# Starting one batch's attention steps earlier and sending another batch's output through the DMA crossbar, in a fused attention and SwiGLU kernel

## The chip, the cores and the metric

The kernel runs on one core of one Trainium2 chip. The core has a matrix engine (PE, with its weight loads shown apart as PEld), a vector engine (DVE), a scalar engine (ACT), a general engine (POOL, GpSimd) and a queue engine (SP, SyncE) that here only issues DMAs. Each engine runs its own instructions in program order and waits for others by semaphores. Matmul results go to PSUM, eight banks per partition; DVE and ACT read them from there. The metric is device microseconds of one launch. The kernel before takes 372.36 us, the median of nine runs that lie between 371.16 and 373.12 us.

## What is computed

Eight batches of eight heads, sequence 576, head width 64: attention with a mask (a band of 32 positions to each side, and eight global positions that see and are seen by all), then a SwiGLU feed-forward block over all 4608 tokens:

```python
scores = scale * np.matmul(q, k.transpose(0, 1, 3, 2))
mask = (np.abs(pos[:, None] - pos[None, :]) <= 32) | is_global[:, None] | is_global[None, :]
attn = softmax(np.where(mask, scores, -1e9))
x = np.matmul(attn, v).transpose(0, 2, 1, 3).reshape(B * S, H * D)   # 4608 x 512
g = x @ w_gate                                                        # 512 -> 1536
out = (g * sigmoid(g) * (x @ w_val)) @ w_out                          # 1536 -> 512
```

Inputs and output are float32; the matmuls work on bf16.

## The kernel before, in words

**The feed-forward block sets the beat.** The 4608 tokens are cut into nine chunks of 512. A chunk is 16 units: twelve `gate` units (each four matmuls into `pg` and four into `pv`, line 704, then a tanh on ACT, line 735, and two DVE operations, `gv` and `h`, lines 737 and 741) and four `outp` units (twelve matmuls into `po`, line 748, a scaling copy on ACT, line 753, a DMA to the output, line 755). The last loop of the kernel runs these 144 units in order, and after unit n it runs the list `gaps[n]`. All attention work of batches 1 to 7, the loads of later batches and three pieces left over from batch 0 stand in these gaps. The program order so written is the order on every engine; nothing is reordered by a scheduler.

**One batch of attention** is a list of steps: `step_T(hp)` transposes k and q of a head pair on PE (batches 1 and 2 only; later batches are cast to bf16 in DRAM by `cast_qk` and transposed by a DMA, `transpose_qk`); `step_GT`, `step_SG`, `step_S2`, `step_P2T` and `step_AV2` handle the global positions; `step_S(u)` makes the scores of the band in five tiles (matmuls, line 492; exp on ACT, line 500; times the band on DVE, line 506, giving `pt`); `step_AV(tp)` multiplies by v in four tiles of 128 rows (lines 540 and 549) and then normalises on DVE (lines 521, 526, 527), giving `xa`; `step_AV8` does the last 64 rows; `step_X(tp)` and `step_X8` transpose `xa` into `xT`, the input of the feed-forward block. For batches below `XB` the transposes of `step_X` are PE matmuls (line 598, 617) and an ACT copy (604, 623); from `XB` on they are DMA transposes issued by SP (lines 587, 610). `xa` has three buffers.

**Where the steps stand.** Before the loop the whole of batch 0 runs, except `step_S(4)`, `step_AV8` and `step_X8`, which stand in gaps 0, 2 and 3. The first two gates of chunk 0 are computed in parts between batch 0's last steps. Batch 1 has its `step_T` in gaps 4, 5 and 6 (two in 6), its scores to `step_AV(0)` in gaps 7 to 11, `step_X(3)` in gap 15 with chunk 1 starting right behind it, `step_AV8` and `step_X8` in gaps 16 and 17. Batch 2 starts in gap 16 and ends in gap 30. Chunk 1 needs batch 1's tokens, chunk 2 needs the first three tiles of batch 2.

**PSUM.** Three pools share the eight banks: `pf` has four single banks (tag `f`: gates, outputs, and batch 0's small tiles), `psc` (tag `sc`) and `pm` (tag `m`) have one pair of two banks each. A step that takes a pair waits until the readers of the pair's last tile have finished. `step_S` uses `sc` except tile 2 of batch 0; `step_T` uses `sc` except `hp` 3; `mtile`, which serves `step_GT`, `step_P2T`, `step_AV2`, `step_X` and `step_X8`, is `m` for every batch but 0.

**Queues.** POOL issues all loads that cast (`load_qk_part`, `load_v`, `cast_qk`, the weights), the gathers of the global rows, and computes their masks (`gather_mask`). SP issues, in this order, batch 2's shifted copy of v (`load_vb`), batch 3's DMA transposes of k and q, and then chunk 1's four output DMAs.

## Time and profile before

| | us |
|---|---|
| median of nine runs | 372.36 |
| lowest, highest | 371.16, 373.12 |
| the profiled execution's own time | 370.23 |
| its span from the first to the last instruction | 368.5 |
| PE busy in the span | 351.0 |
| PE idle in the first 20 us, and from 20 to 40 us | 8.23, 2.77 |
| PE idle from 40 to 300 us, as the windows give it | 2.4 |
| last matmul's end to the end of the span | 4.0 |

The busy time of PE is an upper bound for its work, since matmuls overlap and their ends are modelled; starts are exact. In a timeline row the first number is the start, the second the length, then engine, line, operation, `output<-inputs`, shape, count; a bracket tells how long the engine was idle before the row and what ended it. "Gap n" below is the list after unit n; in this execution gap 2 lies at 32.7 us, gap 11 at 55.3, gap 15 at 69.4, gap 24 at 92.5, gap 30 at 111.3.

### The profile page before, as it was taken

To read this page: it belongs to the slowest core of one execution; us is meant where nothing else is said; L and a number is where in the kernel's file an instruction comes from. 1 tells how busy PE (TensorE), PEld (TensorE's weight loads), DVE (VectorE), ACT (ScalarE), POOL (GpSimd) and SP (SyncE) were. 2 spreads that over 40 slices of the span, in tenths; PEclk is the share of its full clock that TensorE was granted. 3 is DMA by queue.
4 is the path that set the end of the run, shared out by engine and by line. 5 is a ranking of instruction groups with operands and counts; after the bars stand their busy time and mean duration, and the time that the engine had idled before them with its cause. 6 is when DMAs were issued, how large, how long until landed. Compare 5 with 4: busy or idle time off the path is not lost.

```text
span 368.5 us, 7982 instructions
## 1 busy us (share of the span) xinstructions
PE 351.0 (95%) x3294; PEld 175.0 (47%) x3294; DVE 239.0 (65%) x473; ACT 152.7 (41%) x237; POOL 97.5 (26%) x114
## 2 busy tenths in 40 slices
PE   3788999999999999999999999999999999999995
PEld 2565545554454444444444454444544454444442
DVE  6676885288833885488548854886488637815840
ACT  5644573357423552255225532552254233323321
POOL 7947547570227002450246013200000000000000
PEclk9999999999999999999999999999999999999999
DMA  7999999999959996999999998932330131011002
GB/s 103 147 212 203 186 222 169 181 180 150 118 84 121 173 102 110 116 154 143 147 148 144 153 138 136 170 72 60 112 87 2 44 114 24 0 59 58 0 30 85
DMA packets 138996, 42.92 MB, mean 116 GB/s; under 512 B 123856, under 2 KB 133072, under 8 KB 138960
## 3 DMA queue, kind: packets, MB, share of 16 engines
q0 software_dynamic: 93824, 19.40, 64.0%
q1 hardware_dynamic: 45136, 23.01, 30.7%
q8 instruction: 26, 0.43, 0.5%
q14 instruction: 10, 0.08, 0.1%
HBM read 38.28 MB, written 15.34 MB: 145 GB/s over the span
## 4 chain that ended last, share of the span: by engine, by line
PE 84%; DVE 7%; ACT 3%; DMA 3%; issue 1%; POOL 0%; SPq 0%; DVEq 0%; POOLq 0%
PE po L748 26%; PE pg L704 23%; PE pv L704 22%; PE ps_av L540 3%; PE ps_s L492 2%; PE ps_av L549 2%; ACT pe L500 2%; DVE pt L506 2%; DMA vb<-va 2%; PE ps_t L374 1%; DMA k_bf<-in_k_dram 1%; DVE h L741 1%; DVE gvt L468 1%; DVE gv L737 1%; PE ps_x L598 1%
## 5 line engine op out<-in xcount | busy, mean ns | idle before, releaser
L704 PE MATMUL pg<-xT,wg_sb 128*128 128x512 bf16 x424 | 109.3, 380 | 1.2 <-ACT xT L604 0.7
L704 PE MATMUL pv<-xT,wv_sb 128*128 128x512 bf16 x424 | 108.8, 379 | 0.0
L735 ACT ACTIVATE th<-pg 128x512 bf16<-128x512 f32 x108 | 64.4, 597 | 81.6 <-PE pg L704 78.7
L748 PE MATMUL po<-wo_sb,h 128*128 128x512 bf16 x432 | 97.4, 380 | 0.0
L737 DVE SCALAR_TENSOR_TENSOR gv<-th,pg 128x512 bf16<-128x512 bf16 x108 | 74.0, 685 | 34.5 <-ACT th L735 33.9
L741 DVE TENSOR_TENSOR h<-gv,pv 128x512 bf16<-128x512 bf16 x108 | 74.3, 688 | 12.0 <-PE pg L704 0.5
L704 PEld LDWEIGHTS <-wv_sb 128*128 128x128 bf16 x424 | 41.5, 98 | 50.0
L102 POOL DMA_DIRECT2D va<-in_v_dram x40 | 35.1, 962 | 109.0 <-PE ps_av L549 80.4
L748 PEld LDWEIGHTS <-h 128*128 128x128 bf16 x432 | 40.8, 98 | 47.5
L704 PEld LDWEIGHTS <-wg_sb 128*128 128x128 bf16 x424 | 37.2, 98 | 42.0 <-issue 2.9
L753 ACT ACTIVATE osb<-po 128x512 f32<-128x512 f32 x36 | 21.5, 597 | 85.8 <-PE po L748 80.9
L500 ACT ACTIVATE pe<-ps_s 128x1024 bf16<-128x1024 f32 (+1 forms) x40 | 37.4, 939 | 17.2 <-PE ps_s L492 16.6
L506 DVE TENSOR_TENSOR pt<-pe,band 128x1024 bf16<-128x1024 bf16 (+1 forms) x40 | 25.5, 637 | 23.0 <-ACT pe L500 22.9
L521 DVE TENSOR_REDUCE den<-ps_av 128x8 f32<-128x16 f32 (+1 forms) x40 | 6.7, 169 | 36.7 <-PE ps_av L549 35.3
L527 DVE TENSOR_TENSOR xa<-ps_av,den 128x512 bf16<-128x512 f32 (+1 forms) x40 | 25.5, 638 | 1.4
L540 PE MATMUL ps_av<-gvt,pg 128*64 128x264 bf16 x128 | 18.1, 296 | 1.0 <-DVE gvt L476 1.0
L549 PE MATMUL ps_av<-vb,pt 128*64 128x66 bf16 x256 | 17.7, 198 | 1.2 <-DMA vb<-va 1.2
L549 PEld LDWEIGHTS <-pt 128*64 128x64 bf16 x512 | 17.6, 114 | 1.6 <-DMA vb<-va 1.4
L492 PEld LDWEIGHTS <-kT 64*128 64x128 bf16 x576 | 11.3, 98 | 14.4 <-issue 13.6
L549 PE MATMUL ps_av<-va,pt 128*64 128x66 bf16 x256 | 17.8, 198 | 0.0
L492 PE MATMUL ps_s<-qT,kT 64*128 64x64 bf16 x576 | 16.0, 197 | 0.0
L109 POOL DMA_DIRECT2D qf<-in_q_dram x5 | 14.1, 2826 | 0.0
(113 smaller groups left out, 219.8 us busy)
## 6 DMA issues: line engine op xcount, KB each, us to landing
out_dram<-osb SPq DMA_DIRECT2D x36, 256.0 KB, 2.0
vb<-va SPq DMA_DIRECT2D x14, 264.0 KB, 4.5
va<-in_v_dram POOLq DMA_DIRECT2D x24, 128.0 KB, 5.2
kf<-in_k_dram POOLq DMA_DIRECT2D x5, 576.0 KB, 13.1
qf<-in_q_dram POOLq DMA_DIRECT2D x5, 576.0 KB, 20.8
k_bf<-in_k_dram POOLq DMA_DIRECT2D x6, 288.0 KB, 11.9
q_bf<-in_q_dram POOLq DMA_DIRECT2D x6, 288.0 KB, 12.6
va<-in_v_dram POOLq DMA_DIRECT2D x16, 96.0 KB, 5.9
```

Of the source, the lines that this page charges most:

```text
L102: nc.gpsimd.dma_start(out=va[lo:hi, u, :, 0:D], in_=vs[t0 + lo : t0 + hi])
L492: nc.tensor.matmul(out=ps[:, par, 64 * slot : 64 * slot + 64], lhsT=kT[r : r + 64, hp, 64 * t : 64 * t + P], rhs=qTs[b][r : r + 64, hp, 64 ...
L500: nc.scalar.activation(out=pe, in_=ps[:, :, 0 : 64 * ns].rearrange("p r (s c) -> p r s c", c=64), func=AF.Exp, scale=SCALE,)
L506: mult = lambda: nc.vector.tensor_tensor(out=pt.rearrange("p r s c -> p (r s) c"), in0=pe.rearrange("p r s c -> p (r s) c"), in1=bc(band, ...
L527: nc.vector.tensor_tensor(out=xa.rearrange("p (g h) d -> p g h d", g=g), in0=bc(ps, pst + [[1, D]]), in1=bc(den, [[4, g], [1, 4], [0, D]]) ...
L540: nc.tensor.matmul(out=ps[64 * e : 64 * e + 64, hg], lhsT=st["pg"][:, P * tp + 64 * e : P * tp + 64 * e + 64], rhs=st["gv"].rearrange("p h ...
L549: nc.tensor.matmul(out=ps[64 * e : 64 * e + 64, hg, hl, :], lhsT=pt[:, hl % 2, 4 * (hl // 2) + 2 * (tp % 2) + e, :], rhs=(va if e == 0 els ...
L704: nc.tensor.matmul(out=ps[:, 0:n], lhsT=w[:, cc, P * fc : P * (fc + 1)], rhs=xT[:, cc, t0 : t0 + n], start=(cc == 0), stop=(cc == NCC - 1),)
L735: nc.scalar.activation(out=th[:, 0:n], in_=pg[:, 0:n], func=AF.Tanh, scale=0.5)
L737: nc.vector.scalar_tensor_tensor(out=gv[:, 0:n], in0=th[:, 0:n], scalar=1.0, in1=pg[:, 0:n], op0=ALU.add, op1=ALU.mult,)
L741: nc.vector.tensor_tensor(out=st["h"][:, fc, 0:n], in0=gv[:, 0:n], in1=pv[:, 0:n], op=ALU.mult)
L748: nc.tensor.matmul(out=po, lhsT=st["h"][:, fc, P * ts : P * (ts + 1)], rhs=wo_sb[:, fc, :], start=(fc == 0), stop=(fc == NFC - 1),)
```

## The change

Part by part:

- **Batch 0's score tiles and outputs.** `step_S(3)` moves to the pair `m`, which `step_S(2)` uses as well; `step_AV` and `step_X` of batch 0 swap pairs. One warming matmul (`warm(1)`, 512 columns of ones) is put behind each of `step_AV(1)` and `step_AV(2)`.
- **Gate 2 of chunk 0** takes the pair `m` in place of two banks of `pf`.
- **Batch 1** starts in gap 2: `step_T` in gaps 2, 3, 4 and 5, every later step one gap before its old place, `step_X(3)` in gap 14, `step_AV8` in 15, `step_X8` in 16. Batch 0's `step_AV8` and `step_X8` go to gaps 3 and 4.
- **Batch 2** starts in gap 15 and ends in gap 29; each step is one gap earlier. Its loads, gathers and masks move by one to three gaps, and its masks now stand on POOL ahead of batch 3's casts.
- **`step_T`** takes the two pairs in turn (`m` for odd `hp`).
- **`XB` is 2**: batch 2's output goes to `xT` by six DMA transposes on SP, behind batch 3's k and q transposes and around chunk 1's output DMAs, instead of 18 PE transposes and five ACT copies. `step_AV8` of batch 2 keeps its pair.
- **The last output tile of the kernel** is computed in two halves of 256 columns, each with its own bank, ACT copy and DMA.

```diff
-    XB = 3
+    XB = 2
@@ step_T
-            pool, tag = (pm, "m") if hp == 3 else (psc, "sc")
+            pool, tag = (pm, "m") if hp % 2 else (psc, "sc")
@@ step_S
-            pool, tag = (pm, "m") if b == 0 and u == 2 else (psc, "sc")
+            pool, tag = (pm, "m") if b == 0 and u in (2, 3) else (psc, "sc")
@@ step_AV
-            pool, tag = (psc, "sc") if tp % 2 and b == 0 or tp and b in (1, 2) else (pm, "m")
+            if b == 0:
+                pool, tag = (pm, "m") if tp % 2 else (psc, "sc")
+            elif b < XQ:
+                pool, tag = (psc, "sc") if tp else (pm, "m")
+            else:
+                pool, tag = pm, "m"
@@ step_AV8
-            if b >= XB:
+            if b >= XQ:
@@ step_X
-                pool, tag = ((pm, "m"), (psc, "sc"))[tp % 2]
+                pool, tag = ((psc, "sc"), (pm, "m"))[tp % 2]
@@ attention(0)
-                L(step_AV, 1), M("p*", 3), M("xa*", 1), L(step_X, 0),
-                L(step_AV, 2), M("xa*", 2), L(step_X, 1), L(step_AV, 3), M("xa*", 3),
+                L(step_AV, 1), L(warm, 1), M("p*", 3), M("xa*", 1), L(step_X, 0),
+                L(step_AV, 2), L(warm, 1), M("xa*", 2), L(step_X, 1), L(step_AV, 3), M("xa*", 3),
@@ attention(1), attention(2)
-        if b == 1:
-            return [
-                [], [], [], [L(step_GT)], [L(step_T, 0)], [L(step_T, 1)],
-                [L(step_T, 2), L(step_T, 3), vb],
-            ] + mid, end
         if b < XQ:
             return [
-                [L(step_T, 0)], [L(step_T, 1)], [L(step_GT), L(step_T, 2)], [L(step_T, 3), vb],
-            ] + mid, end
+                [L(step_T, 0)], [L(step_T, 1)], [L(step_T, 2), L(step_GT)], [L(step_T, 3), vb],
+            ] + mid + end
@@ gate
+            if t0 == 0 and fc == 2:
+                pair = pm.tile([P, 2, CH], FP32, tag="m", name="pgv")
+                pg, pv = pair[:, 0], pair[:, 1]
@@ outp
+        def outp_last(ts):
+            po = pf.tile([P, DM], FP32, tag="f", name="po")
+            po2 = pf.tile([P, DM], FP32, tag="f", name="po")
+            r0 = t0 + P * ts
+            for i, ps in enumerate((po, po2)):
+                c = slice(DM // 2 * i, DM // 2 * (i + 1))
+                for fc in range(NFC):
+                    nc.tensor.matmul(
+                        out=ps[:, 0 : DM // 2], lhsT=st["h"][:, fc, P * ts : P * (ts + 1)],
+                        rhs=wo_sb[:, fc, c], start=(fc == 0), stop=(fc == NFC - 1),
+                    )
+                osb = ffnw.tile([P, DM], FP32, tag="osb", name="osb", bufs=6)
+                nc.scalar.mul(out=osb[:, 0 : DM // 2], in_=ps[:, 0 : DM // 2], mul=0.5)
+                nc.sync.dma_start(out=out[r0 : r0 + P, c], in_=osb[:, 0 : DM // 2])
@@ the gaps
-    first, last = attention(1)
-    gaps = dict(enumerate(first))
+    gaps = {i: [] for i in range(9)}
     for i, g in enumerate([s4, av8, x8]):
-        gaps[i + (i > 0)] = g + gaps[i + (i > 0)]
+        gaps[(0, 3, 4)[i]] += g
-    cast_at, tr_at, v_at, g_at, m_at = {3: 12, 4: 25}, {3: 22}, {2: 10}, {2: 8}, {2: 15}
-    at(7, qk_now, 2)
-    two, two_end = attention(2)
-    for i, g in enumerate(last):
-        gaps[16 + i] = g
-    for i, g in enumerate(two + two_end):
-        gaps[16 + i] = gaps.get(16 + i, []) + g
+    cast_at, tr_at, v_at, g_at, m_at = {3: 12, 4: 25}, {3: 20}, {2: 8}, {2: 6}, {2: 12}
+    at(5, qk_now, 2)
+    for b, o in ((1, 2), (2, 15)):
+        for i, g in enumerate(attention(b)):
+            gaps[o + i] = gaps.get(o + i, []) + g
```

## The prediction, made before the changed kernel was run

> **What bounds the kernel now.** First I read the busy times by stage, to learn which engine sets the end in each. The columns are the window, its length, then the busy time (and count) of PE, PEld, DVE, ACT, POOL, the granted clock, the DMA share (1 is all 16 engines busy) and GB/s.

> ```profile
> 0.00:20.00 20.00, 11.77 (x209) 7.58 (x211) 13.34 (x50) 11.96 (x17) 17.31 (x30) 1.00 1.18 130
> 20.00:40.00 20.00, 17.23 (x222) 11.30 (x222) 13.64 (x30) 7.87 (x14) 10.42 (x15) 1.00 1.30 206
> ...
> 90.00:100.00 10.00, 9.31 (x128) 5.10 (x127) 8.79 (x20) 5.11 (x8) 1.75 (x2) 1.00 2.08 128
> ...
> 200.00:300.00 100.00, 99.43 (x921) 47.95 (x920) 68.51 (x132) 40.34 (x61) 7.35 (x9) 1.00 0.65 99
> 300.00:368.50 68.50, 64.46 (x325) 29.27 (x322) 34.62 (x54) 19.70 (x33) 0.00 (x0) 0.99 0.12 42
> ```

> From 40 us on PE is idle 2.4 us before the tail, so an edit gains there only by removing PE work or one of the few waits. The head (idle 8.2 + 2.8 us) and the tail (4.0 us) hold the rest. Between 90 and 100 us DVE is nearly as full as PE.

> Second, PE's rows with idle time in the stretch that changes (a bracket gives the idle time before the row and what ended it):

> ```profile
> 24.17 0.22 PE L549 MATMUL ps_av<-vb,pt 128*64 128x66 bf16 x1 [1.20 <-DMA vb<-va]
> 30.99 1.02 PE L704 MATMUL pg<-xT,wg_sb 128*128 128x512 bf16 x4 [0.51 <-DVE gv L737]
> 33.51 0.32 PE L576 MATMUL ps_av<-va,pt 128*64 128x66 bf16 x8 [0.40 <-DVE pt L506]
> 70.69 1.02 PE L704 MATMUL pg<-xT,wg_sb 128*128 128x512 bf16 x4 [0.71 <-ACT xT L604]
> 96.02 0.40 PE L598 MATMUL ps_x<-ident,xa 128*128 128x128 bf16 x4 [0.69 <-DVE xa L527]
> ```

> They are: batch 0's third `step_AV` waiting for the DMA copy of v; gate 2 waiting for a `pf` bank; batch 0's `step_AV8` waiting for its scores; chunk 1's first gate waiting for batch 1's last tile; batch 2's first `step_X` waiting for DVE's normalising. These 2.31 us without the first are what the change can remove.

> Third, the chain that ended last around 93 us, because the wait at 96.02 is only its visible end:

> ```profile
> 92.32 0.60 DVE pt L506
> 92.93 0.61 DVE gv L737
> ...
> 94.32 0.60 DVE pt L506
> ...
> 95.28 0.70 DVE xa L527
> 95.98 0.05 issue
> 96.02 0.40 PE ps_x L598 x4
> ```

> DVE is on the chain without a break from 87.3 to 96 us. In a stretch of gates with `step_AV` in the gaps DVE is the bound, and PE work taken out there is only partly gained.

> **The change, part by part, against the profiled execution (370.23 us, span 368.5).** The build of the changed kernel has 8 PE instructions fewer (18 transposes less, 12 matmuls and 2 warming ones more, two instructions each).

> *1. Head, scores and warming.* Tile 3 of batch 0 must now wait until ACT's exp has read tile 2. In the trace the two tiles' matmuls run together at 17.98 and the two exps at 18.63 (1.94 us). Now: tile 2 until 18.5, its exp until 19.65, tile 3 until 20.3, its exp until 21.4. Between lie two warming matmuls at half rate; `step_AV(0)` starts at 21.15 instead of 19.91. Behind it on DVE are `xa` 0 (until 23.3), tile 3's `pt` (23.95) and `xa` 1 (25.0 instead of 23.8). The third `step_AV` still meets the DMA's landing at 24.13, which covers most of this delay, but `step_X(1)` can start at 25.0 instead of 24.66: **+0.4**. If the DMA came earlier, the cover would be gone and the whole 1.2 us would show. The two `warm(1)` (0.22 us each) fall into these waits.

> [...] These are PE rows before and after some 22 us:

> ```profile
> 18.94 1.04 PE L333 MATMUL ps_w<-ones 128*128 128x512 bf16 x2
> 19.91 0.43 PE L540 MATMUL ps_av<-gvt,pg 128*64 128x264 bf16 x2
> 22.64 0.30 PE L540 MATMUL ps_av<-gvt,pg 128*64 128x264 bf16 x2
> ```

> The same pair of matmuls takes 0.43 and then 0.30 us, although the page's granted clock shows 9 tenths or more throughout. [...] In the trace the switch falls between 21.6 and 22.6, after nearly gapless work from 17.98. By the row alone it stays there, and part 1 costs 0.4. [...]

> *2. Gate 2 in its own pair.* Its last reader is `step_X(3)`'s copy (until 29.14), long done: **-0.5**, the wait at 30.99.

> *3. Batch 1 two gaps earlier.* `step_AV8` moves behind gate 3; its scores are on DVE until 33.46: **-0.4**. `step_T(0)` in gap 2 begins at about 32.6 and needs both loads:

> ```profile
> 20.37 0.73 POOL L80 DMA_DIRECT2D q_bf<-in_q_dram x1
> DMA to landing us min/median/max: 5.5/12.6/12.6
> ```

> 20.37 + 12.6 = 32.97; the k transposes (0.31) come first, so about **+0.1** (0.5 if part 1 costs nothing). Heads 4 to 7 were issued at 21.77 and 25.07 and have to be there only by 38 us. Batch 1's v and its shifted copy landed by 51.9; `step_AV(0)` comes to 53: covered by 1 us. The pairs in turn make `step_GT` wait for `step_T(1)`'s copies one gate earlier, and `step_T(3)` for `step_GT`'s copy: about 0.5 us to spare by DVE's rows, nothing.

> *4. `step_X(0)` of batch 1* now stands behind gate 11 (1.73 us) and not behind an output unit (2.59). That is exactly where batch 2 stood, same steps, same DVE lag (2.3 us from scores to `xa`): **+0.7**.

> *5. Chunk 1's start.* `step_X(3)` gets 2.6 us of output matmuls between itself and the gate: **-0.7**. Gap 15's steps ask for nothing late.

> *6. Gap 16.* `step_X8` of batch 1 and `step_T(1)` of batch 2 now follow each other in pair `m`. From the rows of 75.12 (PE) and 75.44 (ACT, 0.37): `step_T(1)` could start at 75.87 instead of 75.33: **+0.5**, a new PE wait on ACT's copy.

> *7. Batch 2 by the crossbar.* A `step_X` takes 0.32 us of PE, `step_X8` 0.11. From `step_AV(0)` on, at its old times: before, `step_AV(3)` ends at 102.53. Now `step_AV(1)` runs at 95.26, but `step_AV(2)` shares pair `sc` with it and waits for `xa` 1, which DVE finishes at 98.4 as before; then 98.45, gate, `step_AV(3)` at 100.9, end 101.5. So 1.0 for the first three, not 3 x 0.32 + 0.69 + 0.26 = 1.9; then 0.32 + 0.11 for the last two: **-1.5**. The ACT copies (5, 0.58 or 0.37 each) were under PE anyway. SP takes six transposes more, 1.2 us of issue each, behind batch 3's transposes (issued until 86.7) and before or between chunk 1's outputs, which nobody awaits. Landing:

> ```profile
> DMA to landing us min/median/max: 2.3/3.3/6.1
> ```

> `xa` has three buffers, so DVE's `xa` 3 (about 100.6 on the new clock) waits for the first one's landing (issued about 94.1): 6.5 us, just above the longest seen. The DMA share of 2.08 there is the span's highest. Chunk 2 needs three tiles 10 us later. Taken as 0; the fourth rival is its other end. POOL's queue: batch 2's masks (0.39 each) now precede batch 3's casts, whose k and q land by 93 and serve at 118: covered by 25 us.

> *8. Two gaps with PE work fewer* (28, not 30); a gate's row beside a gap is 0.97 instead of 0.86: **-0.2**.

> *9. The tail.* The last matmul, copy (0.60) and DMA (365.12, landed 367.13) are in series. A copy of 256 columns takes 0.37: -0.23. [...] I take -0.1. PE: 24 x 0.109 against 12 x 0.216, nothing. Together **-0.3**.

> Sum: 0.4 - 0.5 - 0.4 + 0.1 + 0.7 - 0.7 + 0.5 - 1.5 - 0.2 - 0.3 = **-1.9 us**: 368.3 for the profiled execution. That one was faster than all nine timed runs, by 2.1 us against their median; I take the difference over to the median: 372.36 - 1.9 = 370.4 (own range 369.4 to 371.5).

> **Rivals.** (a) *The waits only move*: DVE is as late for `step_AV(2)` as it was for `step_X`, part 7 gives only 0.4, and part 1 costs 0.9. For it: DVE's unbroken chain. Against: `xa` 1 ends at 98.4 by rows that the change leaves alone. -0.3: 372.0.

> (b) *The timed runs lose time in the head that the profile doesn't show.* [...] Against: the profiled execution shows no such thing. -1.9 - 1.6: 368.9.

> (c) *The crossbar does not take PE out of the way*, because chunk 2's first gate waits for the tiles. Needs a landing 10 us late; +0 to 1: 371.5. Unlikely.

> (d) *Slower: the first crossbar transpose lands late.* Place: DVE's `xa` 3; behind it in DVE's order are gate 27's `gv` and `h`, and the first output unit of chunk 1 needs that `h` for its twelfth matmul, about 1.3 us after it would be ready. So landing beyond 7.8 us after issue costs PE 1:1, and beyond 9.7 us the whole is slower. Batch 3's transpose of k, 4.5 times the size, took 14.6 us at 72 us under like load. At 12 us: -1.9 + 4.2 = +2.3: 374.7.

> **How the numbers follow.** Chances: forecast 0.52, (a) 0.18, (b) 0.14, (c) 0.04, (d) 0.12. A measurement of this kernel tells 0.2%, 0.75 us, from no change, so faster means under 371.6. Faster: most of the forecast (0.50), all of (b), some of (a) and (c) (0.10): 0.74. Same: the rest of these: 0.14. Slower: (d): 0.12. The range leaves out (d) and the lower half of (b): 368.6 to 372.7.

> **What would show it.** Right: no PE idle before gate 2, `step_AV8` and chunk 1's first gate; a wait of 0.7 before `step_X(0)` of batch 1 on DVE; 0.5 on ACT's `xT` before `step_T(1)` near 73 us; 0.8 on DVE's `xa` before batch 2's `step_AV(2)`; crossbar landings of 3 to 6 us near 95; span about 366.6. Wrong: PE rows at half rate beyond 23 us, a DVE wait on a DMA near 100 us, or a wait for loads in gap 2 above 0.5.

## The result, and the profile after

The changed kernel takes 368.72 us (median of 10 runs, 367.87 to 371.13) against 372.35 us (31 runs, 370.0 to 374.39): ratio 0.9911, 95% interval 0.9887 to 0.9936. Measured again later it took 368.85 us against 371.72 us, ratio 0.9927 (0.9907 to 0.9948). So it gains 2.9 to 3.6 us where 1.9 was forecast, and its median lies on rival (b)'s 368.9 and not on the forecast's 370.4. The profiled execution, however, is only 0.4 us faster than that of before: 369.81 us, span 368.1. Both facts need an explanation, and in both PE at half rate in the head takes part.

First the windows of the changed kernel, in the columns used above.

```profile
20.00:40.00 20.00, 19.15 (x242) 12.33 (x240) 11.99 (x27) 7.81 (x13) 10.05 (x15) 1.00 1.30 206
90.00:100.00 10.00, 9.34 (x123) 4.79 (x122) 9.40 (x21) 4.08 (x6) 2.00 (x3) 1.00 2.23 148
...
300.00:368.10 68.10, 65.04 (x339) 30.76 (x337) 34.71 (x54) 19.88 (x34) 0.00 (x0) 1.00 0.12 43
```

Between 20 and 40 us PE is now busy 19.15 us (17.23 before), and between 90 and 100 us DVE has 9.40 of 10 us: it is the bound there, as forecast. Behind 300 us PE is idle 3.1 us, not 4.0. Next, PE's rows at the places that the prediction named.

```profile
19.10 0.61 PE L492 MATMUL ps_s<-qT,kT 64*128 64x64 bf16 x16 [1.12 <-ACT pe L500]
...
24.42 0.26 PE L554 MATMUL ps_av<-vb,pt 128*64 128x66 bf16 x1 [0.47 <-DMA vb<-va]
...
28.04 0.85 PE L726 MATMUL pv<-xT,wv_sb 128*128 128x256 bf16 x4
28.95 0.60 PE L726 MATMUL pg<-xT,wg_sb 128*128 128x256 bf16 x4
...
32.54 0.39 PE L708 MATMUL pgv<-xT,wg_sb 128*128 128x512 bf16 x1
...
58.31 0.40 PE L603 MATMUL ps_x<-ident,xa 128*128 128x128 bf16 x4 [0.67 <-DVE xa L527]
...
73.00 1.04 PE L708 MATMUL pg<-xT,wg_sb 128*128 128x512 bf16 x4
...
75.47 0.45 PE L374 MATMUL ps_t<-ident,k_bf 96*64 96x96 bf16 x12 [0.46 <-ACT xT L628]
...
98.57 0.30 PE L545 MATMUL ps_av<-gvt,pg 128*64 128x264 bf16 x2 [0.66 <-DVE xa L527]
```

The new wait for ACT at 19.10, gate 2 and chunk 1 without a wait, the waits at 58.31, 75.47 and 98.57: all stand where they were expected. Two rows are new: the wait for `vb` has shrunk from 1.20 to 0.47 us, and the gates' parts run slowly up to 28.6 us (0.85, then 0.60 us for the same work; from a part's `pg` to its `pv` PE takes 0.83 us ahead of the grant at 28.54 and 0.43 behind it), where PE of before was at full speed from 22.4. The tail was and is this copy, of a whole tile before and of half a tile now, each followed by one DMA:

```profile
364.50 0.60 ACT L753 ACTIVATE osb<-po 128x512 f32<-128x512 f32 x1 [1.99 <-PE po L748]
...
365.08 0.38 ACT L761 ACTIVATE osb<-po 128x256 f32<-128x256 f32 x1 [0.93 <-PE po L756]
```

**Where the time went, by segments of PE's starts.** "Grant" is the moment at which the trace records full clock for good. The segments run from the start of batch 0's third score tile (17.98 us before, 17.37 in the changed kernel's first profile) to the first part of a gate, from there to gate 2, from there to chunk 2's first gate, and from there to the end of the span.

| profiled execution | own time | grant | tile to gate part | to gate 2 | to chunk 2 | to the end |
|---|---|---|---|---|---|---|
| before | 370.23 | 22.43 | 7.75 | 5.26 | 83.05 | 254.48 |
| changed | 369.81 | 28.54 | 9.83 | 5.33 | 81.99 | 253.58 |
| changed, second profile | 368.89 | 25.41 | 8.60 | 4.68 | 82.43 | 253.57 |
| `XB` = 3 | 369.58 | 22.10 | 8.29 | 4.68 | 83.06 | 254.40 |
| before, filled hole | 370.16 | 22.12 | 7.85 | 5.26 | 83.13 | 254.47 |
| before, another profile | 372.13 | 27.20 | 8.61 | 5.63 | 83.88 | 254.47 |
| experiment 2 | 371.36 | 28.87 | 9.08 | 5.73 | 82.61 | 254.61 |
| experiment 4 | 369.46 | 23.48 | 8.69 | 4.68 | 82.85 | 254.38 |

The changed kernel's first profile lost 2.1 us between its third score tile and gate 2, most of it to half rate; it had started that tile 0.6 us earlier, and it won 1.1 and 0.9 us behind. Rows with a late grant are no worse kernels: the grant moves from execution to execution of the same code.

### The profile page after: what moved, and what is told of

Same layout as the page of the kernel before. It is cut to its first block, busy times and chain, and to the rows that moved or that the text cites. A ratio compares the mean times of both kernels' runs of the same rounds, so it can differ in the third digit from the quotient of the medians.

```text
span 368.1 us, 7991 instructions
## 1 busy us (share of the span) xinstructions
PE 352.6 (96%) x3290; PEld 176.4 (48%) x3290; DVE 238.9 (65%) x473; ACT 150.8 (41%) x233; POOL 96.9 (26%) x114
## 4 chain that ended last, share of the span: by engine, by line
PE 80%; DVE 11%; ACT 3%; DMA 3%; issue 1%; POOL 0%; SPq 0%; DVEq 0%; POOLq 0%
PE po L769 25%; PE pg L708 22%; PE pv L708 21%; PE ps_av L545 3%; DVE pt L506 3%; ACT pe L500 2%; DVE h L745 2%; PE ps_av L554 2%; PE ps_s L492 2%; DVE gv L741 2%; DMA vb<-va 2%; DMA k_bf<-in_k_dram 1%; DVE gvt L468 1%; PE ps_t L374 1%; PE ps_s L426 1%
## 5 line engine op out<-in xcount | busy, mean ns | idle before, releaser
L769 PE MATMUL po<-wo_sb,h 128*128 128x512 bf16 x420 | 94.6, 379 | 0.0
L769 PEld LDWEIGHTS <-h 128*128 128x128 bf16 x420 | 39.8, 98 | 46.7 <-DVE h L745 0.4
L506 DVE TENSOR_TENSOR pt<-pe,band 128x1024 bf16<-128x1024 bf16 (+1 forms) x40 | 25.4, 636 | 20.1 <-ACT pe L500 20.1
L527 DVE TENSOR_TENSOR xa<-ps_av,den 128x512 bf16<-128x512 f32 (+1 forms) x40 | 25.5, 638 | 1.4
L554 PE MATMUL ps_av<-va,pt 128*64 128x66 bf16 x256 | 18.5, 201 | 0.0
## 6 DMA issues: line engine op xcount, KB each, us to landing
k_bf<-in_k_dram POOLq DMA_DIRECT2D x6, 288.0 KB, 12.6
```

Source lines behind the costliest of these rows:

```text
L506: mult = lambda: nc.vector.tensor_tensor(out=pt.rearrange("p r s c -> p (r s) c"), in0=pe.rearrange("p r s c -> p (r s) c"), in1=bc(band, ...
L527: nc.vector.tensor_tensor(out=xa.rearrange("p (g h) d -> p g h d", g=g), in0=bc(ps, pst + [[1, D]]), in1=bc(den, [[4, g], [1, 4], [0, D]]) ...
L554: nc.tensor.matmul(out=ps[64 * e : 64 * e + 64, hg, hl, :], lhsT=pt[:, hl % 2, 4 * (hl // 2) + 2 * (tp % 2) + e, :], rhs=(va if e == 0 els ...
L769: nc.tensor.matmul(out=po, lhsT=st["h"][:, fc, P * ts : P * (ts + 1)], rhs=wo_sb[:, fc, :], start=(fc == 0), stop=(fc == NFC - 1),)
```

## The experiments

The theory was rival (b): timed runs of before lose time in the head that its profiled execution doesn't show, because PE works at half rate longer. The rival theory was that only the steps of the sum count, and that the timed runs' spread has nothing to do with the hole before the third `step_AV`.

**1. Before, with the hole filled.** Three warming matmuls in the place where PE of before is about to wait for `vb`.

```diff
-L(step_AV, 1), M("p*", 3), M("xa*", 1), L(step_X, 0),
+L(step_AV, 1), M("p*", 3), M("xa*", 1), L(step_X, 0), L(warm, 3),
```

> The kernel before with three more warming matmuls behind batch 0's first step_X, which fill PE's 1.2 us wait for the copy of v. Theory G (the half rate of PE lasts longer in most timed runs of the kernel before than in its profiled one, because of that hole): the median falls by 1 to 2.5 us, to about 370.5, and the runs lie closer together. Rival S (the gain is all removed waits, PE work and tail; nothing in the head): 0 to +0.6 us, since the added matmuls cost up to 0.65 us and remove nothing.

Measured: 370.16 us, 369.77 to 370.48 in 7 runs, beside 371.75 for before; ratio 0.9958 (0.9942 to 0.9974). Adding work that computes nothing makes the kernel 1.6 us faster and takes away its spread. PE's row:

```profile
24.03 0.22 PE L549 MATMUL ps_av<-vb,pt 128*64 128x66 bf16 x1 [0.69 <-DMA vb<-va]
```

The wait is 0.69 us instead of 1.20. Segment by segment the profile equals that of before within 0.1 us, and its own time that of before's profile (370.16, 370.23). So the filling doesn't speed up an execution that was good already; it is the others that get faster.

**What the timed runs' clocks say.** Each timed run comes with the mean clock that PE was granted over its span. It has steps: 0.997 to 1.000, 0.993 to 0.995, and 0.989 to 0.991. In the trace of experiment 5a's first kernel full clock lasts 3.41 us, is taken away and comes back 17.07 us later, five times as long; with half rate in between (0.51 in its row from 10 to 20 us) its mean is 0.977. So half rate for one such window of 3.41 us out of some 368 takes off 0.5 x 3.41 / 368 = 0.005. The traces also show the clock withdrawn behind the last matmul, which takes off up to 0.003 (before's profile has 0.998, the second one of experiment 5 0.997, both with the clock unbroken up to there). So the steps are read here as no, one and two windows of half rate between the first grant and the last matmuls; a late first grant leaves no mark in this number (the changed kernel's first profile, with the grant at 28.54, has 1.000). Counted over the timed runs, the profiled executions of the changed kernel and of the edits among them (the wait for `vb` is that of the kernels' profiles):

| kernel | wait for `vb` | runs | none lost | one | two |
|---|---|---|---|---|---|
| before, two chips | 1.20 | 59 | 13 | 35 | 11 |
| before, the chip of experiment 5 | under 0.2 | 18 | 13 | 3 | 2 |
| before, filled hole | 0.69 | 7 | 7 | 0 | 0 |
| changed (both measurements) | 0.47, under 0.2 | 28 | 26 | 2 | 0 |
| experiments 2 to 4 and the first of 7 | 0.40 or less | 33 | 31 | 2 | 0 |
| the second of 5a | under 0.2 | 7 | 4 | 2 | 1 |
| warming matmuls moved (6, and with 7) | 1.34, 1.60 | 29 | 16 | 13 | 0 |

On the chip of the second measurement, the 12 runs of before with none lost have a median of 370.05 us, the 22 with one lost 371.62, the 8 with two 372.90. The changed kernel: 368.82 with none (15 runs), 371.20 in the single run with one. The edit of experiment 6 has 368.67 (10 runs) and 369.76 (9 runs). So a lost window goes with 1.1 to 1.6 us more, and in the single run with 2.4; by the sum above 3.41 us at half rate take 1.7 at most, so that run lost something else too. With none lost the change gains 370.05 - 368.82 = 1.2 us; of the 2.9 us between the medians the other 1.6 go with windows that it no longer loses.

On one chip filling the hole by 0.5 us took the runs with a lost window from 16 of 17 to none of 7; on another, opening it again in the changed kernel (experiment 6) brought them from 1 of 16 to 9 of 19. The timed runs have no trace, so that the lost windows lie at this hole is inferred and not seen. Nor are they the whole story: three of the 12 runs with none lost took 372.64 to 372.69 us, and on the chip of experiment 5 most runs of before lose none and still have a median of 372.17.

**2. The changed kernel without its two single warming matmuls.**

```diff
-L(step_AV, 1), L(warm, 1), M("p*", 3), M("xa*", 1), L(step_X, 0),
-L(step_AV, 2), L(warm, 1), M("xa*", 2), L(step_X, 1), L(step_AV, 3), M("xa*", 3),
+L(step_AV, 1), M("p*", 3), M("xa*", 1), L(step_X, 0),
+L(step_AV, 2), M("xa*", 2), L(step_X, 1), L(step_AV, 3), M("xa*", 3),
```

> The changed kernel without the two single warming matmuls. Theory G: PE has holes of 0.3 to 1 us again near 23 us, the half rate lasts longer in some runs, the median rises by 0.5 to 2 us against the changed kernel's 368.7 and the spread widens. Rival S: -0.4 to 0 us.

Measured: 369.55 us (367.92 to 371.36, 6 runs), ratio 0.993 (0.9904 to 0.9955). The median is 0.7 to 0.8 us above the changed kernel's and the spread is wide, as the theory expected, but the interval overlaps that of the changed kernel, and no run lost a window. The profiled execution is the slowest of the six (371.36): its grant came at 28.87 us, and its last DMA took 2.74 us to land where the changed kernel's took 1.69. Whether the two matmuls bring the first grant forward, six runs don't tell. The wait for `vb` is short without the two as well, under 0.2 us in this execution, where half rate delays PE too. What is left to shorten it in every execution is part 1's delay: because tile 3 of the scores now waits 1.12 us for ACT, `step_AV(0)` to `step_AV(2)` come later, and PE reaches `vb` when it has nearly landed.

**3. The changed kernel with batch 2's output on PE again** (`XB = 3`).

> The changed kernel with batch 2's output by PE transposes and ACT copies again. By the sum of the prediction (part 7): +1.5 us, about 370.2, with a PE wait of 0.7 before batch 2's first step_X. If the crossbar's transposes cost something elsewhere (rival d): less than +0.5.

Measured: 369.94 us (369.31 to 371.36, 10 runs, none with a lost window), ratio 0.9954 (0.9937 to 0.9971). Against the changed kernel's runs without a lost window (368.63 and 368.82 in its two measurements) that is 1.1 to 1.3 us, across chips, where 1.5 was expected. In the table the same: to chunk 2 it needs 83.06 us, exactly what before needed, and the changed kernel 81.99. So all the moving of steps between gate 2 and chunk 2 nets nothing, and the crossbar's 1.07 us are the gain there.

```profile
94.00 0.28 PE L603 MATMUL ps_x<-ident,xa 128*128 128x128 bf16 x2 [0.66 <-DVE xa L527]
```

The wait on DVE's `xa` is 0.66 us here, and 0.66 in the changed kernel at 98.57, before `step_AV(2)`: with the crossbar it stands one step later and is as long. DVE sets both.

**4. The changed kernel with its last output tile whole.**

```diff
-            if t0 + CH == NT and ts == 3:
-                return outp_last(ts)
```

> The changed kernel with the last output tile in one piece. By the prediction (part 9): +0.3 us. By the two profiles, whose last matmul ends 0.6 us later and whose span ends 0.4 us earlier: +0.9 to +1.0 us. Theory G and rival S say nothing different here.

Measured: 369.24 us (368.33 to 371.15, 7 runs), ratio 0.9935 (0.9911 to 0.9959). The profiles put 254.38 against 253.58 us from chunk 2 to the end, so 0.8 us; the medians of runs without a lost window (369.06 against 368.63 and 368.82) say 0.2 to 0.4, within their spread. The traces show the parts. From the last matmul's end to the end of the span, before takes 4.06 us and the changed kernel 3.07: copy and issue 0.2 less, the DMA from issue to landing 0.3 less (2.01 to 1.69), and 0.5 less behind the landing (1.39 to 0.93). In that last piece SP goes through eight DMA semaphores one after the other, some 0.06 us each; that of the last DMA comes first in this order before, and last after, so that nothing is left to go through when it lands. The change adds seven DMAs to SP's order (six crossbar transposes and the second half), which moves the last one on by seven in the cycle of eight. In this experiment, with one DMA fewer than the changed kernel, it comes seventh, and the end follows the landing by 0.99 us though the tile is whole; the DMA itself took 2.27 us here. With `XB` = 3 it comes second: six semaphores follow its landing, SP's next step comes another 0.37 us later, and the segment takes 254.40 us though the tile is halved. So the 0.5 comes from the number of SP's DMAs, not from the halving.

**5. Before, two more profiles**, unaltered.

> The kernel before, unchanged, profiled once more, to see when PE's rows change to full speed. Theory G: in an execution that takes about 372 us the change comes at 26 us or later (its first profile: 22.4 us, and 370.2 us); in one of about 370 us near 22 us. Rival S: the change stays near 22 us whatever the time.

> The same once more: the kernel before, unchanged. Theory G: time and moment of the change to full speed go together again. Rival S: they do not.

Measured: 371.57 and 372.13 us, grants at 24.07 and 27.20. The second has the late grant that the theory wants, the first hardly; neither loses a window afterwards, and neither has the wait for `vb`. Both show something else: ACT's copy in gap 17 starts long after the transposes that it reads. Here it is in before's first profile and then in the second of these two:

```profile
76.07 0.64 ACT L379 COPY kT<-ps_t 128x576 bf16<-128x576 bf16 x1 [0.26 <-PE ps_t L374]
...
78.37 0.64 ACT L379 COPY kT<-ps_t 128x576 bf16<-128x576 bf16 x1 [1.48 <-PE pg L704]
```

In the second, PE's rows end the transposes at 77.10, but the trace has PE's semaphore event only at 78.35. It costs PE 0.8 us two steps on (`step_T(2)` waits for DVE's copy). The same lateness at the score tiles has PE wait 0.7 to 1.4 us for ACT before `step_AV(0)`, so that it comes to `vb` when that has landed. It appears in all four profiles taken on this chip, the next two experiments among them, and in none of the other ten. Its cause stays open. It makes these two profiles poor evidence for or against the clock, and it leaves open how much of before's 372.2 us on this chip it makes up, where 13 of 18 timed runs lost no window.

**5a. On the same chip, two changes of the changed kernel's head.** First ten warming matmuls ahead of everything.

```diff
-L(squares), L(tables_a),
+L(warm, 10), L(squares), L(tables_a),
```

> The changed kernel with ten warming matmuls ahead of everything, in the 6 us in which PE waits for the first load (some 4.3 us at half rate from 1.5 us on). Theory G: PE's rows run at full speed from 6 to 9 us on, the late change near 23 to 29 us is gone, and the median falls by 0.5 to 1.5 us below the changed kernel's. Rival S: no difference within 0.4 us, since PE waits for loads and for ACT and DVE until 24 us.

Measured: 370.12 us (369.8 to 371.69, 12 runs), ratio 0.9939 (0.9917 to 0.9962). The changed kernel itself was not timed on this chip; against its 368.7 and 368.85 elsewhere this is no gain, against the expectation. The windows of this kernel, columns as above:

```profile
0.00:10.00 10.00, 7.01 (x80) 3.37 (x82) 6.48 (x34) 4.96 (x7) 8.06 (x17) 1.00 0.71 100
10.00:20.00 10.00, 6.32 (x129) 4.03 (x123) 6.56 (x16) 5.64 (x9) 9.25 (x14) 0.51 1.63 159
20.00:30.00 10.00, 8.87 (x128) 6.48 (x128) 5.53 (x15) 3.79 (x5) 2.24 (x4) 0.64 1.23 216
```

The column before the DMA share is the granted clock. Full clock was granted at 6.79 us and taken away at 10.20, 3.41 us or one window later; it came back at 27.27, five windows later. In the first of these windows PE waits twice:

```profile
8.11 0.70 PE L354 MATMUL ps_t<-ident,q_bf 96*64 96x96 bf16 x24 [0.67 <-DMA q_bf<-in_q_dram]
9.56 0.70 PE L354 MATMUL ps_t<-ident,k_bf 96*64 96x96 bf16 x24 [0.76 <-DMA k_bf<-in_k_dram]
```

So the clock was lost again behind a window with 1.4 us idle of 3.41. Here a trace shows a loss of the kind that the timed runs of before only let one infer; the mean clocks (0.976 to 0.981) say that 11 of the 12 timed runs lost four or five windows so. The idle time alone doesn't decide: before's profile kept the clock through a window with 1.2 us idle behind its grant, that of experiment 6 through one with 1.5, and that of 7 with 6 through one with 1.6. What else counts (the kind of work in the window, or where it begins) stays open.

Second, the scores' and outputs' pairs of batch 0 as before, the warming matmuls kept.

```diff
-            pool, tag = (pm, "m") if b == 0 and u in (2, 3) else (psc, "sc")
+            pool, tag = (pm, "m") if b == 0 and u == 2 else (psc, "sc")
...
-                pool, tag = (pm, "m") if tp % 2 else (psc, "sc")
+                pool, tag = (psc, "sc") if tp % 2 else (pm, "m")
...
-                pool, tag = ((psc, "sc"), (pm, "m"))[tp % 2]
+                pool, tag = ((pm, "m"), (psc, "sc"))[tp % 2]
```

> The changed kernel with batch 0's score tile 3 in its old pair (and the pairs of batch 0's output tiles as before), all else as changed. By the prediction's part 1: -0.4 us (no wait of 1.1 us for ACT near 19 us). Theory G: a gapless PE from 17.4 to 22.9 us makes the change to full speed earlier, up to -1 us more. If the new pairs help for another reason: slower by up to 0.5 us.

Measured: 370.0 us (368.11 to 370.36, 7 runs), ratio 0.993 (0.9902 to 0.9959). It was expected to gain, since part 1's delay is gone; beside the 370.12 of the first edit on the same chip it doesn't. 3 of its 7 runs lost windows (one of them two). But its profile has no wait for `vb`, because ACT's late signals hold PE up ahead of it, so those windows can't be laid to that hole, and seven runs on this chip decide nothing on part 1's delay.

**6. The two warming matmuls moved into PE's wait for ACT**, on one chip with another profile of the changed kernel.

```diff
-L(step_S, 2), L(step_S, 3), L(warm, 2), L(step_AV, 0),
+L(step_S, 2), L(warm, 2), L(step_S, 3), L(step_AV, 0),
```

> The changed kernel once more, unaltered, beside the next three on one chip. If the moment at which PE goes to full speed changes from execution to execution and sets the spread, the profiled execution's own time follows that moment: with full speed from 28.6 us it was 369.8; before 24.5 us it must be 368.4 to 369.0, and chunk 2 must start near 113.4 instead of 114.5. If the spread has another source, the own time does not go with it. Median 368.5 to 369.1.

> The two warming matmuls stand between batch 0's third and fourth score tile, where PE waits 1.12 us for ACT in the changed kernel, instead of behind the fourth: no work is added, and the longest hole of the head is filled. Theory (holes near 20 us put off full speed in many runs): 0.3 to 0.8 below the changed kernel and a narrow spread. Rival (only the length of PE's order counts; DVE's xa sets the head's end): 0 to -0.2, the same spread.

Measured: the changed kernel 368.85 us (16 runs; profiled with the grant at 25.41, own time 368.89, chunk 2 at 113.62: the earlier grant goes with the shorter time, as expected), the edit 368.90 us (367.7 to 370.82, 19 runs), ratio 0.9939 (0.9919 to 0.9959). No gain, and a wider spread. The hole was moved, not removed:

```profile
24.68 0.22 PE L554 MATMUL ps_av<-vb,pt 128*64 128x66 bf16 x1 [1.34 <-DMA vb<-va]
```

The 1.12 us at 19 are gone, `step_AV(0)` is earlier, and PE waits 1.34 us for `vb` behind the grant (22.34). Nine of its 19 runs lost a window, against one of the changed kernel's 16 on the same chip. This was made against the theory's first wording (any hole near 20 us), which falls: the hole at 19 us does the median no visible harm, and the one that the edit opens at 24 us, behind the grant, goes with lost windows. It also shows that `vb`'s landing bounds the head here: a grant 3 us earlier changed the own time by 0.07 us.

The second profile of the changed kernel has one wait that the first hadn't, first on DVE, then on PE:

```profile
101.81 0.69 DVE L527 TENSOR_TENSOR xa<-ps_av,den 128x512 bf16<-128x512 f32 x1 [0.48 <-DMA xT<-xa]
```

```profile
102.56 0.29 PE L492 MATMUL ps_s<-qT,kT 64*128 64x64 bf16 x8 [0.41 <-DVE xa L527]
```

That is rival (d)'s place, exactly: DVE's fourth `xa` waits for the first crossbar transpose, which landed 6.96 us after its issue (6.24 in the first profile, 5.3 to 7.2 over nine). The four landings beyond 6.6 us (6.94, 6.96, 6.98, 7.20) had PE wait 0.39, 0.41, 0.42 and 0.65 us: one to one. The last of them is experiment 4's:

```profile
102.32 0.29 PE L492 MATMUL ps_s<-qT,kT 64*128 64x64 bf16 x8 [0.65 <-DVE xa L527]
```

**7. The pairs of the transposes of k and q as before**, alone and with the edit of 6.

```diff
-            pool, tag = (pm, "m") if hp % 2 else (psc, "sc")
+            pool, tag = (pm, "m") if hp == 3 else (psc, "sc")
```

> The changed kernel with the pairs of the transposes of k and q as before (only the last head pair in m). Theory of part 6 (the second head pair's transposes wait 0.46 us for ACT's copy of the tile that shares pair m): that wait is gone and nothing takes its place: -0.4 to -0.5 against the changed kernel. Rival (the pair in turn is what lets the transposes run on; two following ones in pair sc now wait for each other's copies): 0 to +0.5.

> Both of the last two edits together. Theory: their gains add, since they lie at 20 and 75 us: 0.7 to 1.2 below the changed kernel, 367.5 to 368.0. Rival: no more than one of them remains, 368.2 to 368.8.

Measured: alone 368.44 us (367.79 to 370.7, 10 runs), ratio 0.992 (0.9893 to 0.9947), 0.4 below the changed kernel on that chip; with 6 368.89 us (367.22 to 369.5, 10 runs), 0.9922 (0.9897 to 0.9947), 4 of 10 with a lost window: the gains don't add, against the expectation. The wait at 75 us is gone, as expected. In its place batch 1 has a new one:

```profile
36.02 0.28 PE L374 MATMUL ps_t<-ident,k_bf 96*64 96x96 bf16 x4 [0.36 <-DVE qT L383]
```

The theory thus holds in batch 2 and its rival in batch 1, and the profiles (81.79 us to chunk 2 against 81.99 and, with the crossbar's 0.41, 82.43) leave 0.2 us that is the edit's own. The lowest median of all is this kernel's, but the intervals don't part it from the changed kernel. Turns for batch 1 and the old pairs for batch 2 should keep both gains; that wasn't tried.

## Why the prediction was right in direction and short in size

**The step that failed** is the last of the sum: "I take the difference over to the median". The 2.1 us between before's profile and its median were treated as a constant that the changed kernel would have too. On the chip of the second measurement 1.6 us of the 2.9 gained go with windows of half rate that most runs of before lose (46 of 59 on two chips) and the changed kernel nearly never does (2 of 28); on the chip of experiment 5, where before rarely loses one, what makes up its median stays open. Rival (b) said nearly this (as experiment 1's expectation puts it, the half rate lasts longer, where the clocks show it come back), gave 368.9, and was held at 0.14, with "the profiled execution shows no such thing" against it. But one profile was one draw, of the fewer runs that lose nothing; nine timed runs all slower than it said so. The 1.6 us in its sum was an estimate that no run shows ahead of the experiments; these put 1.1 to 1.6 us, and once 2.4, beside a lost window. So 368.72 lies below the forecast's own range (369.4 to 371.5), and just inside the whole one (from 368.6) only because half of rival (b) was in it. The clue "granted clock 9 tenths or more throughout" was no clue either: the trace's record of the clock begins with the first grant, and what comes ahead is shown as full (the changed kernel's row from 20 to 40 us has 1.00, with the grant at 28.54).

**Part by part.** Part 1: +0.4 forecast; with a grant at 22.1 (`XB` = 3) the segment takes 8.29 us, not 7.75: +0.5. The 0.9 that rival (a) puts for it is shown by no run ahead of the prediction; the changed kernel's second profile, granted at 25.41, took 8.60 us, +0.85, and its first, granted at 28.54, 9.83 us, 1.5 more than with `XB` = 3. The same delay is what shrinks the wait for `vb`, so the step that was booked as a loss goes with the largest gain of the change on the chip of the second measurement; no step of the sum had that. Part 2: 5.26 to 4.68 us at full clock, 0.6 for the 0.5 forecast. Part 3: no wait before `step_AV8`, and q's first half landed at 33.12, ahead of its use at 34.65, because the head of this execution ended late. The +0.1 was no empty fear: in experiment 4, where PE came to it at 32.8, it cost 0.44:

```profile
33.25 0.45 PE L374 MATMUL ps_t<-ident,q_bf 96*64 96x96 bf16 x12 [0.44 <-DMA q_bf<-in_q_dram]
```

Part 4: 0.67 for 0.7. Part 5: none, as forecast. Part 6: 0.46 for 0.5. Parts 3 to 6 together: +0.2 forecast, 0.0 measured (83.06 against 83.05, with what `XB` = 3 keeps of part 8 in it). Parts 7 and 8: -1.7 forecast, -1.07 measured with the landing in time and -0.6 with it late; the wait that takes the place of `step_X`'s is 0.66 where 0.8 was allowed, so by elimination the PE work under DVE's chain was credited too high. Part 9: -0.3 forecast, -0.9 in the profile, 0.5 of it behind the landing, which the sum didn't count. No run shows the 0.1 that its sum takes for the DMA of half the bytes; measured from issue to landing were 2.01 and 1.69 us, 0.3 less. The sum of the measured parts, 0.5 - 0.6 + 0.0 - 1.1 - 0.9 = -2.1, comes near the -1.9 by luck: the errors of parts 7 and 8 (+0.6) and of part 9 (-0.6) cancel. In the medians of runs with no lost window it is 1.2 (370.05 against 368.82): the crossbar's late landing takes 0.4 of the difference where it happens, and the grant's moment, which no timed run tells, may take the rest.

**The rivals.** (a) was right that DVE comes as late for `step_AV(2)` as it did for `step_X` (0.66 us), but part 7 gave 0.6 to 1.1 and not 0.4, and the waits of parts 2 and 5 left and did not come back. (c): chunk 2's tiles landed by 105 us, 9 us ahead of it. (d) has the right place, but its threshold was 6.6 us after issue and not 7.8, since not the twelfth output matmul but batch 3's score tile, which stands earlier, waits for that `xa`; landings up to 7.2 us were seen, so it took 0.65 us at most.

## What to carry to other kernels

Before adding up steps against a profiled execution, ask whether that execution is a typical one: compare its own time and its granted clock with those of the timed runs, and where they differ treat the difference as a mechanism to be explained, not as an offset. In the trace of the early warming two waits of PE's, 0.67 and 0.76 us long and just behind the first grant, went with 17.07 us of half rate: judge such a wait by the clock behind it too, not by its length alone. And before became 1.6 us faster by three matmuls that compute nothing (experiment 1). Moving a hole out of one place is only worth it if the thing that PE waits for next has landed: the 1.12 us taken out at 19 us came back as 1.34 at `vb` (experiment 6).
